# Attention stage of a fused kernel: a fixed engine order, Q's feature map in place on PSUM or on ScalarE, another queue for the s stores, gated FFN loads

## Chip, cores, metric

The kernel runs on 1 core of one Trainium2 chip. The metric is device time in microseconds (us) of one execution. All executions count as fast (within 1.5% of the kernel's fastest), but for one of e5.

## The reference

```python
xn = layernorm(x)                                   # x: 2048 tokens x 1024, bf16
# A: linear attention, 32 heads of 32
q, k, v = split(xn @ wqkv)
phi = lambda t: where(t > 0, t + 1, exp(t)) + 1e-6
kv = einsum("bhsd,bhse->bhde", phi(k), v);  z = sum_s phi(k)
o  = (phi(q) @ kv) / (phi(q) @ z + 1e-6)
s  = o @ wo
# B: gated FFN, F = 3584
g  = silu((silu(xn @ w_gate) * (xn @ w_up)) @ w_down)
out = x + s * g
```

Since `phi(t) = min(exp(t), 1) + max(t, 0) + 1e-6`, it needs no select.

## The kernel before

The code is cut to what the change touches (cuts are marked, and the comments are added here). There are three stages in time: K/V (all of K and V, and the sums `kv` and `z`), attention (Q, numerator/denominator "ND", the transposition of o to oT, and S = oT times wo), and the FFN. Tokens come in four blocks `b` of 512, with four tiles `t` each. GpSimd computes in the background, from the FFN weights, difference tiles T that the FFN needs ("preparations": a weight load, four tensor operations, two stores to DRAM).

```python
    psA = p12.enter_context(tc.tile_pool(name="psA", bufs=3, space=PSUM))
    psB = p12.enter_context(tc.tile_pool(name="psB", bufs=3, space=PSUM))   # q_ps, s_ps, kv_ps
    psC = p12.enter_context(tc.tile_pool(name="psC", bufs=2, space=PSUM))

    def emit_phi(work, t_ps, dst, W, in_place=False):
        e_t = work.tile([P, W], FP32, name="e_t", tag="e_t")
        ex = nc.scalar.activation(out=e_t[:], in_=t_ps, func=ACT.Exp)
        if in_place:                       # used by K from tile 9 on
            r = t_ps
            nc.vector.tensor_scalar(out=r, in0=t_ps, scalar1=0.0, scalar2=EPS, op0=ALU.max, op1=ALU.add)
        else:                              # used by Q
            r_t = work.tile([P, W], FP32, name="r_t", tag="r_t")
            r = r_t[:]
            nc.scalar.activation(out=r, in_=t_ps, func=ACT.Relu)
            nc.vector.tensor_scalar(out=r, in0=r, scalar1=EPS, scalar2=None, op0=ALU.add)
        nc.vector.scalar_tensor_tensor(out=dst, in0=e_t[:], scalar=1.0, in1=r,
                                       op0=ALU.min, op1=ALU.add)
    # ... cut
    def prep(n, after=None):               # one preparation: weight load (SP queue), then GpSimd
        # ... cut
            t = w_slot()
            load_gu(t, key[1], key[2], after)
            emit_T(key, t)                 # 4 gpsimd.tensor_tensor, 2 gpsimd DMA stores
    # ... cut: K/V stage, with one prep per token tile from tile 10 on
        emit_C(NT - 1)
        p1_man.close()                     # end of the explicit order: the scheduler decides from here
        for g in range(G):
            emit_Q(0, g)                   # 8 matmuls of 512 columns, then emit_phi(...)
            if g % 4 == 3:
                prep(1)
    # ... cut
        def emit_OT(b, hf):                # o of two tiles to DRAM, and back transposed
            nc.sync.dma_start(out=rows..., in_=o_blk[:, hf * th:(hf + 1) * th, :])
            nc.sync.dma_start_transpose(out=oT_tiles[b][:, :, hf * tk:(hf + 1) * tk], in_=rows)

        def emit_S(b, t, cc):              # 8 matmuls, one ScalarE copy
            # ... cut
            if cc == NCC - 1:
                nc.gpsimd.dma_start(out=s_dram[r0:r0 + P, :], in_=s_tiles.pop((b, t))[:])

        for b in range(NB):                # fq: Q(b+1), then S(b-1)
            # ... cut
            fill(2)
            for t in range(TPB):
                emit_ND(b, t)
                fill(1 if lastb else 2)
                if t % 2 == 1:
                    emit_OT(b, t // 2)
                    prep(1)
            if b + 1 < NB:
                fill(max(0, len(fq) - 4))
                prep(1)
        # ... then S of what is left, and of the last block
```

Of the kernel before, what the change touches and what calls it, by code (L numbers as in the profile page):

```python
# [21 lines left out]
def kernel(  # L22
# [12 lines left out]
    P = 128  # L35
# [37 lines left out]
    tp = ctx.enter_context(tc.tile_pool(name="tp", bufs=8))  # L73
    p12 = ExitStack()
    psA = p12.enter_context(tc.tile_pool(name="psA", bufs=3, space=PSUM))
    psB = p12.enter_context(tc.tile_pool(name="psB", bufs=3, space=PSUM))
    psC = p12.enter_context(tc.tile_pool(name="psC", bufs=2, space=PSUM))

    SCHED = mybir.DependencyInfo(mybir.DependencyClass.NoSync, mybir.DependencyReason.SCHED_ONLY)
    SYNCD = mybir.DependencyInfo(mybir.DependencyClass.Sync, mybir.DependencyReason.SCHED_ONLY)  # L80
# [45 lines left out]
    def blk_rows_pt(t_dram, b):  # L126
        return t_dram[b * TB:(b + 1) * TB, :].rearrange("(t p) d -> p t d", p=P)

    def emit_phi(work, t_ps, dst, W, in_place=False):
        e_t = work.tile([P, W], FP32, name="e_t", tag="e_t")  # L130
        ex = nc.scalar.activation(out=e_t[:], in_=t_ps, func=ACT.Exp)  # L131
        if in_place:
            r = t_ps
            nc.vector.tensor_scalar(out=r, in0=t_ps, scalar1=0.0, scalar2=EPS, op0=ALU.max, op1=ALU.add)
        else:
# [3 lines that stand above are left out]
            nc.vector.tensor_scalar(out=r, in0=r, scalar1=EPS, scalar2=None, op0=ALU.add)  # L139
        nc.vector.scalar_tensor_tensor(out=dst, in0=e_t[:], scalar=1.0, in1=r,  # L140
                                       op0=ALU.min, op1=ALU.add)
        return ex

    blk12_es = ExitStack()
    blk12 = blk12_es.enter_context(tc.tile_pool(name="blk12", bufs=2, side="right"))
# [4 lines left out]
    def emit_Q(b, g):  # L150
        if b not in pqT_tiles:
            pqT_tiles[b] = blk12.tile([P, G, TB], BF16, name="pqT", tag="pqT")
        pqT = pqT_tiles[b]
        btok = slice(b * TB, (b + 1) * TB)
        q_ps = psB.tile([P, TB], FP32, name="q_ps", tag="B")
        for dc in range(DC):
            nc.tensor.matmul(q_ps[:], lhsT=wq_sb[:, dc, g * P:(g + 1) * P], rhs=xn_ap(dc, btok),  # L157
                             start=(dc == 0), stop=(dc == DC - 1))
        emit_phi(phiw, q_ps[:], pqT[:, g, :], TB)

    NPASS = NB // 2
    passes = list(range(NPASS - 1, -1, -1))
# [8 lines left out]
    w_tiles = {}  # L171
    w_next = [0]
    n_slot = [0]

    def w_slot():
        t = wgu.tile([P, DC, FW], BF16, name="w_sb", tag=("wg_sb" if n_slot[0] % 2 == 0 else "wu_sb"))
# [3 lines left out]
    def load_gu(t, kind, k, after=None):  # L180
        d = nc.sync.dma_start(out=t[:], in_=(wg_v if kind == "g" else wu_v)[:, :, k * FW:(k + 1) * FW])
        gate([d], after, sync=True)

    def load_w(after=None):
        key = w_seq[w_next[0]]
        w_next[0] += 1
        if key in w_tiles:
            return
        p, kind, k = key
        t = w_slot()  # L190
        if kind[0] == "d":
            nc.sync.dma_start(out=t[:].rearrange("p a b -> p (a b)").rearrange("p (k n) -> p k n", k=2),
                              in_=wd_v[:, 2 * k:2 * k + 2, :])
        else:
            load_gu(t, kind, k, after)
        w_tiles[key] = t

    def load_w_to(n):
# [24 lines left out]
    def load_T(key):  # L223
        ta, tb = t_pair()
        for dst, src in zip((ta, tb), t_drams[key[1:]]):
            nc.sync.dma_start(out=dst[:].bitcast(FP32), in_=src[:])
        t_tiles[key] = (ta[:, 1], ta[:, 0], tb[:, 0], tb[:, 1])

    gkeys = [(passes[0], kd, fg) for fg in range(NFG) for kd in ("g", "u")]
# [2 lines left out]
    def prep(n, after=None):  # L232
        for _ in range(n):
            if not prep_q:
                return
            key = prep_q.popleft()
            t = w_slot()
            load_gu(t, key[1], key[2], after)
            emit_T(key, t)
            if key in gkeys[0:2]:  # L240
                w_tiles[key] = t
            else:
                t_tiles.pop(key)

    kvz_ps = [psA.tile([P, GPT, NDW], FP32, name=f"kvz{j}", tag="A") for j in range(NJ)]
    with ExitStack() as p1:
# [248 lines left out]
            if i >= 10:  # L495
                prep(1)
        emit_C(NT - 1)
        p1_man.close()
        for g in range(G):
            emit_Q(0, g)  # L500
            if g % 4 == 3:
                prep(1)

    for j in range(NJ):
        g0 = j * GPT
        ng = min(GPT, G - g0)
        nc.vector.tensor_tensor(out=KVZ[:, g0:g0 + ng, 0:P], in0=kvz_ps[j][:, 0:ng, 0:P],
                                in1=mask[:, None, :].to_broadcast([P, ng, P]), op=ALU.mult)
        nc.vector.tensor_tensor(out=KVZ[:, g0:g0 + ng, P:P + HPG],
                                in0=kvz_ps[j][:, 0:ng, P:P + 1].to_broadcast([P, ng, HPG]),  # L510
                                in1=sel[:, None, :].to_broadcast([P, ng, HPG]), op=ALU.mult)
# [17 lines left out]
    with ExitStack() as p2:  # L529
# [9 lines left out]
        def emit_ND(b, t):  # L539
            pqT = pqT_tiles[b]  # L540
            ttok = slice(t * P, (t + 1) * P)
            if b not in o_blks:
                o_blks[b] = blk.tile([P, TPB, D], BF16, name="o_blk", tag="o_blk")
            o_sb = o_blks[b][:, t, :]
            for j in range(NJ):
                g0 = j * GPT
                ng = min(GPT, G - g0)
                pool_j = psC if j == NJ - 1 and NJ > 1 else psA
                nd_ps = pool_j.tile([P, GPT, NDW], FP32, name="nd_ps", tag=("C" if pool_j is psC else "A"))
                for gi in range(ng):  # L550
                    g = g0 + gi
                    mm = nc.tensor.matmul(nd_ps[:, gi, :], lhsT=pqT[:, g, ttok], rhs=KVZ[:, g, :],  # L552
                                          start=True, stop=True)
                    if j == 0 and gi == 0 and t == 0:
                        marks[("ND", b)] = mm
                rden = small.tile([P, GPT, HPG], FP32, name="rden", tag="rden")
                nc.vector.tensor_scalar(out=rden[:, 0:ng, :], in0=nd_ps[:, 0:ng, P:P + HPG],
                                        scalar1=EPS, scalar2=None, op0=ALU.add)
                nc.vector.reciprocal(out=rden[:, 0:ng, :], in_=rden[:, 0:ng, :])
                nc.vector.tensor_tensor(  # L560
                    out=o_sb[:, g0 * P:(g0 + ng) * P].rearrange("p (g h e) -> p g h e", g=ng, h=HPG),
                    in0=nd_ps[:, 0:ng, 0:P].rearrange("p g (h e) -> p g h e", h=HPG),
                    in1=rden[:, 0:ng, :, None].to_broadcast([P, ng, HPG, DH]),
                    op=ALU.mult)
# [10 lines left out]
        def emit_S(b, t, cc):  # L575
            oT = oT_tiles[b]
            ttok = slice(t * P, (t + 1) * P)
            if (b, t) not in s_tiles:
                s_tiles[(b, t)] = work.tile([P, D], BF16, name="s_sb", tag="s_sb")
            s_sb = s_tiles[(b, t)]  # L580
            s_ps = psB.tile([P, CW], FP32, name="s_ps", tag="B")
            for c in range(G):
                nc.tensor.matmul(s_ps[:], lhsT=oT[:, c, ttok], rhs=wo_sb[:, c, cc * CW:(cc + 1) * CW],  # L583
                                 start=(c == 0), stop=(c == G - 1))
            nc.scalar.copy(out=s_sb[:, cc * CW:(cc + 1) * CW], in_=s_ps[:])  # L585
            if cc == NCC - 1:
                r0 = b * TB + t * P
                nc.gpsimd.dma_start(out=s_dram[r0:r0 + P, :], in_=s_tiles.pop((b, t))[:])  # L588

        fq = deque()  # L590

        def fill(n):
            for _ in range(n):
                if not fq:
                    return
                fq.popleft()()

        for b in range(NB):
            if b + 1 < NB:
                for g in range(G):  # L600
                    fq.append(lambda b=b + 1, g=g: emit_Q(b, g))
            if b > 0:
                for t in range(TPB):
                    for cc in range(NCC):
                        fq.append(lambda b=b - 1, t=t, cc=cc: emit_S(b, t, cc))
            lastb = b == NB - 1
            fill(2)
            for t in range(TPB):
                emit_ND(b, t)
                fill(1 if lastb else 2)  # L610
                if t % 2 == 1:
                    emit_OT(b, t // 2)
                    prep(1)
            if b + 1 < NB:
                fill(max(0, len(fq) - 4))
                prep(1)
        blk_es.close()
        blk12_es.close()
        sp = ctx.enter_context(tc.tile_pool(name="p3S", bufs=1, side="right"))
        emit_Ssum(passes[0])  # L620
        prep(len(prep_q))
        while fq:
            fq.popleft()()
        for t in range(TPB):
            for cc in range(NCC):
                emit_S(NB - 1, t, cc)
    p12.close()

    with ExitStack() as p3:
# [138 lines left out]
        with tc.manual_schedule(engines={mybir.EngineType.PE, mybir.EngineType.DVE, mybir.EngineType.Activation,  # L768
                                         mybir.EngineType.Pool}):
            base = 0  # L770
            for pi, p in enumerate(passes):
# [4 lines left out]
                def get_T(key):  # L776
# [4 lines left out]
                    else:  # L781
                        emit_T(key, w_tiles[key])

                load_w_to(base + 5)
                for i in range(3):
                    get_T(keys[i])
                emit_a(keys[0])
                emit_c22(keys[0])
                for i in range(n):
# [46 lines left out]
```

## Time and profile before

| | before |
|---|---|
| time, median | 830.1 us (829.65 to 830.28) |
| span of the profiled execution | 828.0 us |
| first Q matmul / first FFN matmul | 134.2 / 275.7 us |
| attention, from one to the other | 141.5 us |
| FFN, to the end of the span | 552.3 us |

PE is TensorE, DVE VectorE, ACT ScalarE, POOL GpSimd, SPq the queue of SyncE from which most DMAs are issued. From the page of the kernel before, the busy share in tenths in 40 slices of 20.7 us, and the clock that TensorE was granted:

```profile
PE   6999999579999999999999999999999999999997
DVE  6675436999556276676776027076676776710405
POOL 2471799930101145345380001020000000000200
PEclk9999999769999999999999999999999999999999
```

The two slices with a 5 and a 7 for PE are 145 to 186 us; DVE shows 9 in both, POOL 9 and then 3, and PEclk 7 and 6. The table of stretches gives the same in us (columns: stretch, its length, busy us of each engine with its instruction count, granted clock, DMA share, GB/s):

```profile
140.00:160.00 20.00, 13.27 (x46) 5.11 (x46) 19.90 (x8) 4.34 (x8) 19.94 (x22) 0.77 0.84 291
160.00:180.00 20.00, 11.56 (x45) 4.88 (x44) 18.48 (x27) 6.12 (x12) 13.27 (x15) 0.63 0.60 234
179.20:276.00 96.80, 96.22 (x527) 47.82 (x536) 60.98 (x181) 42.66 (x74) 8.14 (x15) 1.00 0.43 128
```

TensorE is idle or slow in the first two stretches, and full from 179 us on. The chain of waits, in order of time, says who holds it (start, us, what):

```profile
140.22 3.75 DVE r_t L139
...
144.69 5.96 DVE r_t L139
...
151.36 3.75 DVE r_t L139
...
155.83 5.94 DVE r_t L139
...
173.22 6.00 PE q_ps L157 x16
```

These are VectorE's "+EPS" additions to r_t. The same operation on 512 elements takes 0.43 us in the group's median, not 6 us. The last line shows sixteen matmuls in 6.00 us, which take 3.45 us at full clock. The timeline shows what ran beside one of them (start, us, engine, line, operation, out<-in, count):

```profile
144.61 6.03 DVE L139 TENSOR_SCALAR r_t<-r_t 128x512 f32<-128x512 f32 x1
144.75 1.17 POOL L212 TENSOR_TENSOR T_1910<-w_sb 128x512 fp32r<-128x512 bf16 x1
...
145.86 1.16 POOL L214 TENSOR_TENSOR T_1911<-w_sb 128x512 fp32r<-128x512 bf16 x1
...
146.97 1.16 POOL L213 TENSOR_TENSOR T_1910<-w_sb,T_1910 128x512 fp32r<-128x512 bf16 x1
148.09 1.15 POOL L212 TENSOR_TENSOR T_2063<-w_sb 128x512 fp32r<-128x512 bf16 x1
149.20 1.15 POOL L215 TENSOR_TENSOR T_1911<-w_sb,T_1910 128x512 fp32r<-128x512 bf16 x1
...
150.67 0.69 DVE L140 SCALAR_TENSOR_TENSOR pqT<-e_t,r_t 128x512 bf16<-128x512 f32 x1
```

The 6.03 us addition ends 0.3 us after a run of five GpSimd tensor operations has ended (150.64 and 150.35 us), while the K/V stage's in-place form, with its operand in PSUM, isn't touched by the same neighbour (count, then min/median/max in ns):

```profile
L134 DVE TENSOR_SCALAR kv_ps<-kv_ps x14: 700/700/700, 85.0 to 131.4; 128x512 f32<-128x512 f32 x14
```

### The profile page before, as it was taken

The numbers are of one execution on the slowest core, as the hardware profiler recorded it, in microseconds if no ns is written. First come the engines' busy times: TensorE is split into PE (matmuls) and PEld (weight loads), VectorE is DVE, ScalarE is ACT, GpSimd is POOL, SyncE is SP. The second block draws the span as 40 slices with busy tenths as digits, with TensorE's granted clock in tenths as the row PEclk, the third lists the DMA queues.
The fourth block names the chain that finished last, engine by engine and source line by source line (L and its number), as shares of the span: only waits on it lengthen the run. The fifth ranks groups of instructions, "written<-read, shape, count | busy, mean of one in ns | idle before, by whom it ended". The sixth has DMA issues, their size and how long they took to land.

```text
span 828.0 us, 10023 instructions
## 1 busy us (share of the span) xinstructions
PE 794.4 (96%) x3736; PEld 434.3 (52%) x3808; DVE 475.1 (57%) x728; ACT 221.5 (27%) x364; POOL 214.4 (26%) x325
## 2 busy tenths in 40 slices
PE   6999999579999999999999999999999999999997
PEld 3544444135544666666665444456666666644443
DVE  6675436999556276676776027076676776710405
ACT  4544333245343322322222011032322222200102
POOL 2471799930101145345380001020000000000200
PEclk9999999769999999999999999999999999999999
DMA  9249978834525377877878538569777777754541
GB/s 325 82 150 228 308 274 283 314 145 130 153 89 178 115 245 237 275 230 242 272 232 294 181 118 320 165 189 364 252 247 252 247 258 241 252 200 152 204 152 51
DMA packets 149760, 178.92 MB, mean 216 GB/s; under 512 B 30928, under 2 KB 106064, under 8 KB 149712
## 3 DMA queue, kind: packets, MB, share of 16 engines
q1 hardware_dynamic: 137984, 137.25, 52.3%
q0 software_dynamic: 11584, 40.90, 13.8%
q8 instruction: 30, 0.49, 0.2%
q10 hardware_dynamic: 144, 0.13, 0.1%
q14 instruction: 18, 0.15, 0.1%
HBM read 127.93 MB, written 44.04 MB: 208 GB/s over the span
## 4 chain that ended last, share of the span: by engine, by line
PE 87%; DVE 7%; DMA 3%; POOL 2%; issue 1%; ACT 1%; DVEq 0%; ACTq 0%
PE zw L641 25%; PE xb L641 12%; PE y_pd L726 11%; PE y_ps L726 11%; PE kv_ps L408 9%; PE s_ps L583 7%; PE yb L641 6%; PE q_ps L157 5%; DVE r_t L139 3%; DMA xnT<-xn_dram 1%; DMA xn_dram<-xn_blk 1%; PE nd_ps L552 1%; DVE pqT L140 1%; DVE sy L763 0%; DVE stats L322 0%
## 5 line engine op out<-in xcount | busy, mean ns | idle before, releaser
L726 PEld LDWEIGHTS <-hT 128*128 128x128 bf16 x896 | 87.7, 98 | 105.7
L408 PE MATMUL kv_ps<-wkv_sb,xnT 128*128 128x512 bf16 x499 | 114.3, 383 | 2.1 <-DMA xnT<-xn_dram 1.5
L641 PE MATMUL xb<-xnT,w_sb 128*128 128x512 bf16 x420 | 113.7, 380 | 1.5
L726 PE MATMUL y_ps<-w_sb,hT 128*128 128x512 bf16 x440 | 102.5, 379 | 0.4
L726 PE MATMUL y_pd<-w_sb,hT 128*128 128x512 bf16 x438 | 102.0, 379 | 0.5
L763 DVE TENSOR_TENSOR sy<-sy,io 128x512 f32<-128x512 f32 (+1 forms) x33 | 22.2, 671 | 137.6 <-ACT sy L762 137.4
L641 PEld LDWEIGHTS <-w_sb 128*128 128x128 bf16 x672 | 56.8, 98 | 83.1 <-issue 30.5
L766 POOL DMA_DIRECT2D out_dram<-io x24 | 13.0, 543 | 332.5 <-DVE io L764 329.8
L408 PEld LDWEIGHTS <-xnT 128*128 128x128 bf16 x512 | 49.6, 98 | 59.2 <-DMA xnT<-xn_dram 1.9
L157 PE MATMUL q_ps<-xnT,wq_sb 128*128 128x512 bf16 x250 | 64.2, 410 | 10.1 <-ACT r_t L138 9.6
L583 PE MATMUL s_ps<-wo_sb,oT 128*128 128x512 bf16 x249 | 56.0, 379 | 0.4
L698 ACT ACTIVATE sg<-sg 128x1024 f32<-128x1024 f32 x28 | 29.6, 1058 | 97.1 <-DVE sg L694 97.1
L139 DVE TENSOR_SCALAR r_t<-r_t 128x512 f32<-128x512 f32 x50 | 46.0, 920 | 15.4 <-ACT r_t L138 15.1
L762 ACT ACTIVATE sy<-y_pd 128x512 f32<-128x512 f32 x16 | 8.7, 595 | 159.9 <-PE y_pd L726 159.9
L704 DVE TENSOR_TENSOR hT<-cu,sg 128x1536 bf16<-128x1536 f32 x28 | 49.9, 1781 | 0.0
L157 PEld LDWEIGHTS <-wq_sb 128*128 128x128 bf16 x256 | 26.1, 104 | 42.5 <-issue 18.9
L583 PEld LDWEIGHTS <-oT 128*128 128x128 bf16 x256 | 24.8, 98 | 28.8
L588 POOL DMA_DIRECT2D s_dram<-s_sb x16 | 8.7, 543 | 95.4 <-ACT s_sb L585 95.4
L131 ACT ACTIVATE e_t<-q_ps 128x512 f32<-128x512 f32 x32 | 19.1, 597 | 50.2 <-DVE pqT L140 26.0
L641 PE MATMUL zw<-S_2699,w_sb 128*128 128x512 f16 x112 | 29.0, 382 | 0.0
L641 PE MATMUL zw<-S_4632,w_sb 128*128 128x512 f16 x112 | 29.0, 382 | 0.0
L585 ACT CAST s_sb<-s_ps 128x512 bf16<-128x512 f32 x32 | 18.7, 586 | 35.1 <-PE s_ps L583 32.0
(1000 smaller groups left out, 1221.5 us busy)
## 6 DMA issues: line engine op xcount, KB each, us to landing
w_sb<-in_B_w_down_dram SPq DMA_DIRECT2D x56, 512.0 KB, 4.0
w_sb<-in_B_w_gate_dram SPq DMA_DIRECT2D x40, 512.0 KB, 5.2
w_sb<-in_B_w_up_dram SPq DMA_DIRECT2D x28, 512.0 KB, 5.7
o_dram<-o_blk SPq DMA_DIRECT2D x8, 512.0 KB, 2.8
s_dram<-s_sb POOLq DMA_DIRECT2D x16, 256.0 KB, 2.3
io<-in_A_x_dram SPq DMA_DIRECT2D x16, 256.0 KB, 3.4
io<-s_dram SPq DMA_DIRECT2D x16, 256.0 KB, 4.1
xp<-in_A_x_dram SPq DMA_DIRECT2D x15, 256.0 KB, 7.6
```

The lines of the kernel that those rows point to most:

```text
L131: ex = nc.scalar.activation(out=e_t[:], in_=t_ps, func=ACT.Exp)
L139: nc.vector.tensor_scalar(out=r, in0=r, scalar1=EPS, scalar2=None, op0=ALU.add)
L157: nc.tensor.matmul(q_ps[:], lhsT=wq_sb[:, dc, g * P:(g + 1) * P], rhs=xn_ap(dc, btok), start=(dc == 0), stop=(dc == DC - 1))
L408: mm = nc.tensor.matmul(kv_ps[:], lhsT=xn_ap(dc, tok), rhs=wkv_sb[:, dc, c * CW:(c + 1) * CW], start=(dc == 0), stop=(dc == DC - 1))
L583: nc.tensor.matmul(s_ps[:], lhsT=oT[:, c, ttok], rhs=wo_sb[:, c, cc * CW:(cc + 1) * CW], start=(c == 0), stop=(c == G - 1))
L585: nc.scalar.copy(out=s_sb[:, cc * CW:(cc + 1) * CW], in_=s_ps[:])
L641: nc.tensor.matmul(out, lhsT=lhs(k), rhs=rhs(k), start=(first and k == 0), stop=(k == HK - 1), skip_group_check=True)
L698: nc.scalar.activation(out=c[:, 1:3, :], in_=c[:, 1:3, :], func=ACT.Silu)
L704: nc.vector.tensor_tensor(out=hv[:, TB:4 * TB], in0=c[:, 1:4, :].rearrange("p a b -> p (a b)"), in1=sg[:, 1:4, :].rearrange("p a b -> p (a ...
L726: nc.tensor.matmul(ys[(t, c)], lhsT=h[:, fc, tt], rhs=wt[:, o:o + CW], start=(fc == 0), stop=(fc == FC - 1), skip_group_check=True)
L763: nc.vector.tensor_tensor(out=sy[:], in0=sy[:], in1=s_in[:, cs], op=ALU.mult)
L766: eng.dma_start(out=out2[r0:r0 + P, cs], in_=xres[:, cs])
```

## The change

Its intent: no VectorE operation of Q's feature map that GpSimd can lock out; VectorE's load cut in half where ScalarE has room; the whole attention stage in a fixed order, with S(b-1) spread between Q(b+1), and the preparations one by one after each o transposition; the s stores off GpSimd's queue; and the first FFN loads held back until S of the last block begins.

```diff
-    def emit_phi(work, t_ps, dst, W, in_place=False):
+    def emit_phi(work, t_ps, dst, W, in_place=False, act=False):
         e_t = work.tile([P, W], FP32, name="e_t", tag="e_t")
-        ex = nc.scalar.activation(out=e_t[:], in_=t_ps, func=ACT.Exp)
+        if act:
+            nc.scalar.activation(out=e_t[:], in_=t_ps, func=ACT.Relu, scale=-1.0)
+            nc.scalar.activation(out=e_t[:], in_=e_t[:], func=ACT.Exp, scale=-1.0)
+            nc.scalar.activation(out=t_ps, in_=t_ps, func=ACT.Relu)
+            nc.vector.scalar_tensor_tensor(out=dst, in0=e_t[:], scalar=EPS, in1=t_ps,
+                                           op0=ALU.add, op1=ALU.add)
+            return
+        nc.scalar.activation(out=e_t[:], in_=t_ps, func=ACT.Exp)
# emit_Q: psB (3 buffers) becomes ps2 (5 buffers, shared with S and a third of ND), and
-        emit_phi(phiw, q_ps[:], pqT[:, g, :], TB)
+        emit_phi(phiw, q_ps[:], pqT[:, g, :], TB, in_place=True, act=b > 0 or g % 2 == 1)
# ... cut
-            load_gu(t, kind, k, after)
+            load_gu(t, kind, k, after or first_gate[0])
# ... cut: the same gate on the first T loads
+    p2_man.enter_context(tc.manual_schedule(engines={PE, DVE, Activation, Pool, SP}))   # all of attention
# ... cut
-                nc.gpsimd.dma_start(out=s_dram[r0:r0 + P, :], in_=s_tiles.pop((b, t))[:])
+                nc.scalar.dma_start(out=s_dram[r0:r0 + P, :], in_=s_tiles.pop((b, t))[:])
# ... cut: fq and fill are replaced by a list
+        for b in range(NB):
+            q = [q_item(b + 1, g) for g in range(G)] if b + 1 < NB else []
+            sl = sh(b - 1, 0) + sh(b - 1, 1) if b > 0 else []          # the 8 S items of block b-1
+            body = q[:2] + mix(q[2:], sl)
+            at = (1, 4, 7, 10) if len(body) > 12 else ((1, 3, 5, 7) if b == 0 else (0, 1, 2, 3))
+            for k, f in enumerate(body):
+                f()
+                if k in at:
+                    nd_item(b, at.index(k))()       # ND; after an odd tile also emit_OT and prep(1)
# ... cut: then S of the last block
+                if pi == 0:
+                    first_gate[0] = marks[("S", NB - 1, 0)]
                 load_w_to(base + 5)
```

More of the change, by code (lines that the diff above doesn't have):

```diff
@@ L75 @@
     psA = p12.enter_context(tc.tile_pool(name="psA", bufs=3, space=PSUM))
-    psB = p12.enter_context(tc.tile_pool(name="psB", bufs=3, space=PSUM))
-    psC = p12.enter_context(tc.tile_pool(name="psC", bufs=2, space=PSUM))
+    ps1 = ExitStack()
+    psB = ps1.enter_context(tc.tile_pool(name="psB", bufs=3, space=PSUM))
+    psC = ps1.enter_context(tc.tile_pool(name="psC", bufs=2, space=PSUM))
     SCHED = mybir.DependencyInfo(mybir.DependencyClass.NoSync, mybir.DependencyReason.SCHED_ONLY)
@@ L141, in emit_phi @@
                                        op0=ALU.min, op1=ALU.add)
-        return ex
     blk12_es = ExitStack()
@@ L154, in emit_Q @@
         btok = slice(b * TB, (b + 1) * TB)
-        q_ps = psB.tile([P, TB], FP32, name="q_ps", tag="B")
+        q_ps = ps2.tile([P, TB], FP32, name="q_ps", tag="B2")
         for dc in range(DC):
@@ L173 @@
     n_slot = [0]
+    first_gate = [None]
     def w_slot():
@@ L225, in load_T @@
         for dst, src in zip((ta, tb), t_drams[key[1:]]):
-            nc.sync.dma_start(out=dst[:].bitcast(FP32), in_=src[:])
+            gate([nc.sync.dma_start(out=dst[:].bitcast(FP32), in_=src[:])], first_gate[0], sync=True)
         t_tiles[key] = (ta[:, 1], ta[:, 0], tb[:, 0], tb[:, 1])
@@ L497 @@
         emit_C(NT - 1)
-        p1_man.close()
+        ps1.close()
+        ps2 = p12.enter_context(tc.tile_pool(name="ps2", bufs=5, space=PSUM, reuse_waits="tile"))
         for g in range(G):
@@ L502 @@
                 prep(1)
+        p1_man.close()
+    p2_man = ExitStack()
+    p2_man.enter_context(tc.manual_schedule(engines={mybir.EngineType.PE, mybir.EngineType.DVE,
+                                                     mybir.EngineType.Activation, mybir.EngineType.Pool,
+                                                     mybir.EngineType.SP}))
     for j in range(NJ):
@@ L547, in emit_ND @@
                 ng = min(GPT, G - g0)
-                pool_j = psC if j == NJ - 1 and NJ > 1 else psA
-                nd_ps = pool_j.tile([P, GPT, NDW], FP32, name="nd_ps", tag=("C" if pool_j is psC else "A"))
+                if j < NJ - 1:
+                    nd_ps = psA.tile([P, GPT, NDW], FP32, name="nd_ps", tag="A")
+                else:
+                    nd_ps = ps2.tile([P, GPT, NDW], FP32, name="nd_ps2", tag="B2")
                 for gi in range(ng):
@@ L580, in emit_S @@
             s_sb = s_tiles[(b, t)]
-            s_ps = psB.tile([P, CW], FP32, name="s_ps", tag="B")
+            s_ps = ps2.tile([P, CW], FP32, name="s_ps", tag="B2")
             for c in range(G):
-                nc.tensor.matmul(s_ps[:], lhsT=oT[:, c, ttok], rhs=wo_sb[:, c, cc * CW:(cc + 1) * CW],
-                                 start=(c == 0), stop=(c == G - 1))
+                mm = nc.tensor.matmul(s_ps[:], lhsT=oT[:, c, ttok], rhs=wo_sb[:, c, cc * CW:(cc + 1) * CW],
+                                      start=(c == 0), stop=(c == G - 1))
+                marks.setdefault(("S", b, t), mm)
             nc.scalar.copy(out=s_sb[:, cc * CW:(cc + 1) * CW], in_=s_ps[:])
@@ L587, in emit_S, with q_item, s_item, nd_item @@
                 r0 = b * TB + t * P
-                nc.gpsimd.dma_start(out=s_dram[r0:r0 + P, :], in_=s_tiles.pop((b, t))[:])
-        fq = deque()
-        def fill(n):
-            for _ in range(n):
-                if not fq:
-                    return
-                fq.popleft()()
-        for b in range(NB):
-            if b + 1 < NB:
-                for g in range(G):
-                    fq.append(lambda b=b + 1, g=g: emit_Q(b, g))
-            if b > 0:
-                for t in range(TPB):
-                    for cc in range(NCC):
-                        fq.append(lambda b=b - 1, t=t, cc=cc: emit_S(b, t, cc))
-            lastb = b == NB - 1
-            fill(2)
-            for t in range(TPB):
+                nc.scalar.dma_start(out=s_dram[r0:r0 + P, :], in_=s_tiles.pop((b, t))[:])
+        def q_item(b, g):
+            return lambda: emit_Q(b, g)
+        def s_item(b, t, cc):
+            return lambda: emit_S(b, t, cc)
+        def nd_item(b, t):
+            def f():
                 emit_ND(b, t)
-                fill(1 if lastb else 2)
                 if t % 2 == 1:
@@ L613, with mix, sh @@
                     prep(1)
-            if b + 1 < NB:
-                fill(max(0, len(fq) - 4))
-                prep(1)
+            return f
+        def mix(a, b_):
+            r = []
+            for k in range(max(len(a), len(b_))):
+                r += a[k:k + 1] + b_[k:k + 1]
+            return r
+        def sh(b, hf):
+            return [s_item(b, t, cc) for t in (2 * hf, 2 * hf + 1) for cc in range(NCC)]
+        for b in range(NB):
[7 more added lines that the diff above has]
+                    nd_item(b, at.index(k))()
+        b = NB - 1
         blk_es.close()
@@ L621 @@
         prep(len(prep_q))
-        while fq:
-            fq.popleft()()
-        for t in range(TPB):
-            for cc in range(NCC):
-                emit_S(NB - 1, t, cc)
+        for f in sh(b, 0) + sh(b, 1):
+            f()
+    p2_man.close()
     p12.close()
@@ L786 @@
                     get_T(keys[i])
+                first_gate[0] = None
                 emit_a(keys[0])
```

## The prediction

> **What bounds the kernel now.** The chain of waits is 87% TensorE; for the FFN (276 us to 828 us of the span) it is almost nothing else. The exception is the start of attention. Between 137.7 and 173 us the chain's pieces are VectorE's: the "+EPS" TENSOR_SCALAR on r_t, eight times 1.3 to 6.0 us, where its group's median is 0.43 us, and the pqT SCALAR_TENSOR_TENSOR after it. The table of stretches shows TensorE busy 13.3 and 11.6 of 20 us in 140-160 and 160-180, with its clock at 0.77 and 0.63. GpSimd is busy 19.9 and 13.3 of 20 us there: its weight-preparation TENSOR_TENSORs were pulled forward by the scheduler. In the timeline each slow TENSOR_SCALAR ends within 0.4 us of the end of a run of GpSimd tensor operations. The Trainium skill ("SBUF — State Buffer", "Who interferes with whom") says that VectorE in a 2-port mode, or with two SBUF inputs, and GpSimd lock each other out, and that one SBUF input outside such a mode doesn't contend. The trace agrees: the K/V stage's in-place version on PSUM takes 700 ns in all 14 instances, with GpSimd busy beside it.
>
> From 179.2 to 276 us TensorE is 99% busy at full clock: 416 matmuls of 512 columns at 0.216 us plus 15 numerator groups of 0.47 us make 96.9 us, the whole stretch.
>
> **What the change does.**
> - Q's feature map: the 50% of block 0 in place costs VectorE 0.70 + 0.69 us; the rest has one VectorE operation (0.69 us) and three ScalarE ones (about 0.6 us, the second waiting for the first: estimate 1.6 to 1.8 us per group, against 1.73 us of matmuls). No VectorE operation has two SBUF inputs or a 2-port form any more. ScalarE is tight in Q(1) only.
> - Explicit order: preparations 9 to 14 no longer run before attention but after each o transposition, so GpSimd is mostly idle during Q(0).
> - s stores leave GpSimd's queue for ScalarE's.
> - S(b-1) is spread between Q(b+1). oT must arrive earlier: for the first S item I estimate 1 to 3 us of slack (store 2.8 us + transposition 4.2 us after VectorE's 2.7 us), for block 3's first half 0.5 to 1.5 us.
> - FFN loads wait for S of the last block, about 14 us before the FFN: enough for first use.
>
> **Sum.** Attention's TensorE work is 512 x 0.216 + 16 x 0.47 = 118 us. It should start at about 135.2 us (after the last K/V matmuls) and end at about 253.2 us, with 1 to 2 us of small waits at 254.7, where now it ends at 276. Saved: 21.5 us, all on the critical path. Predicted 808.5 us, range 805.5 to 815; faster by over 2% 0.86, within 2% 0.13, slower 0.01.
>
> **What would show it.** TensorE's clock tenths stay at 9 throughout; no VectorE operation in Q(0) over 1 us; about 80 Q matmuls done by 153 us instead of 173; first FFN matmul near 254 us; FFN length unchanged at about 552 us; GpSimd's tensor work in 140-160 us nearly gone.
>
> **What would make it wrong.** S waiting for oT (strict order can't fill that hole); ScalarE's dependent chain taking over 2 us per group, so that Q(1) waits for PSUM; the late GpSimd preparations colliding with the S sums (two SBUF inputs) before the FFN; gated loads arriving late, which would lengthen the FFN's start by several us.

## The result, and the profile after

| | before | after |
|---|---|---|
| time, median | 830.1 us | 815.72 us (814.78 to 817.15) |
| ratio | 1 | 0.9829 (0.981 to 0.9848) |
| first Q / first FFN matmul | 134.2 / 275.7 us | 135.3 / 260.6 us |
| attention | 141.5 us | 125.3 us |
| FFN | 552.3 us | 552.4 us |

A ratio is the mean time of one kernel's fast runs over that of the other's of the same rounds, so it is not quite the ratio of the medians. All outputs are right. The kernel is 1.7% faster, where 2.6% was predicted; 815.7 us lies just outside the range of 805.5 to 815.

The span starts with loads and the K/V stage, which end at slightly different times from one execution to the next (the first Q matmul lies between 134.2 and 139.3 us in all traces but the slow one of e5). Attention's length is therefore the sharper measure. Before it was 141.5 us, and the estimate of pure TensorE work was 118 us.

The slow start is gone. The page's rows of the changed kernel for TensorE and its clock:

```profile
PE   6999999999989999999999999999999999999997
PEclk9999999999998999999999999999999999999999
```

and its stretches:

```profile
140.00:160.00 20.00, 20.00 (x107) 9.55 (x105) 12.50 (x26) 15.46 (x28) 0.00 (x0) 1.00 0.00 0
...
240.00:260.00 20.00, 15.35 (x63) 6.43 (x62) 8.99 (x4) 6.49 (x9) 3.92 (x4) 0.83 0.94 265
```

TensorE is full in 140 to 160 us, at full clock; but 240 to 260 us shows 15.35 of 20 us and a clock of 0.83, which the kernel before did not have. The chain of waits names it:

```profile
161.88 3.90 DMA o_dram<-o_blk
...
165.80 5.19 DMA oT<-o_dram
...
171.03 1.90 PE s_ps L600 x8
...
233.33 3.44 PE s_ps L600 x16
236.77 8.07 DMA oT<-o_dram
...
244.89 16.09 PE s_ps L600 x64
```

Twice the chain runs through the o store and the transposition of oT. At 171 us this is nearly free. At 240.2 us TensorE has done the last S item of block 2 and stands until 244.89 us, since the first half of oT of block 3 lands only then, 8.07 us after its issue. TensorE's waits in this stage (total us, times, longest):

```profile
PE s_ps L600 <- DMA oT<-o_dram: 5.1, 2, 4.7
```

After the hole the clock is down: 64 matmuls take 16.09 us, against 64 x 0.216 = 13.8 us, so 2.3 us more. The stretches show it (columns as above; the granted clock is the third number from the end):

```profile
242.00:244.00 2.00, 0.00 (x0) 0.00 (x0) 0.00 (x0) 0.00 (x0) 0.00 (x0) 0.59 1.21 219
244.00:246.00 2.00, 1.11 (x3) 0.43 (x4) 0.00 (x0) 0.00 (x0) 0.00 (x0) 0.50 1.09 398
...
250.00:252.00 2.00, 2.00 (x11) 0.91 (x10) 2.00 (x2) 0.59 (x1) 0.00 (x0) 1.00 0.88 191
```

The queue's issues around the hole (SPq timeline):

```profile
231.88 0.38 SPq L589 DMA_DIRECT2D o_dram<-o_blk  x1
236.77 4.30 SPq L590 DMA_TRANSPOSE oT<-o_dram  x1
241.58 0.65 SPq L589 DMA_DIRECT2D o_dram<-o_blk  x1
```

The o store of 231.88 took 4.9 us before the transposition could be issued, where before such stores took 2.8 us in the median. While the two were under way, from 231.9 to 244.8 us, so were two T stores of 0.5 MB that GpSimd had issued from 226.3 us on, two more from 236.3 us on, four s stores, and the o store of the second half; the weight load of 224.88 us had landed at 231.6 us.

The sum for attention: 118 us of work, 0.4 us at the first S item, 4.65 us of hole and 2.3 us of low clock make 125.35 us; the trace has 125.3 us.

### The profile page after: what moved, and what is told of

Same layout as the page of the kernel before. It is cut to its first block, busy times and chain, and to the rows that moved or that the text cites. A ratio compares the mean times of both kernels' runs of the same rounds, so it can differ in the third digit from the quotient of the medians.

```text
span 813.0 us, 10086 instructions
## 1 busy us (share of the span) xinstructions
PE 792.4 (97%) x3808; PEld 432.4 (53%) x3808; DVE 446.0 (55%) x700; ACT 236.9 (29%) x388; POOL 205.0 (25%) x309
## 4 chain that ended last, share of the span: by engine, by line
PE 88%; DMA 5%; DVE 3%; POOL 2%; issue 1%; ACT 1%; SPq 0%; DVEq 0%
PE zw L663 25%; PE xb L663 12%; PE y_pd L748 12%; PE y_ps L748 11%; PE kv_ps L417 8%; PE s_ps L600 7%; PE yb L663 6%; PE q_ps L165 4%; DMA oT<-o_dram 2%; DMA xnT<-xn_dram 1%; DMA xn_dram<-xn_blk 1%; DMA xp<-in_A_x_dram 1%; PE kvz L439 1%; PE nd_ps L569 1%; DVE sy L785 0%
## 5 line engine op out<-in xcount | busy, mean ns | idle before, releaser
L663 PE MATMUL zw<-S,T 128*128 128x512 f32 x672 | 175.3, 409 | 0.0
L663 PEld LDWEIGHTS zw<-S,T 128*128 128x128 f32 x672 | 126.4, 188 | 32.3
L682 ACT COPY s<-xb 128x512 f32<-128x512 f32 x56 | 32.7, 584 | 158.4 <-PE xb L663 158.4
L221 POOL TENSOR_TENSOR T<-w_sb 128x512 fp32r<-128x512 bf16 x28 | 32.5, 1161 | 175.1 <-DMA w_sb<-in_B_w_gate_dram 80.2
L683 DVE TENSOR_TENSOR s<-yb,s 128x512 f32<-128x512 f32 x56 | 38.6, 689 | 63.9 <-ACT s L682 63.9
L663 PE MATMUL yb<-S,T 128*128 128x512 f32 x224 | 71.5, 441 | 0.0
L600 PE MATMUL s_ps<-wo_sb,oT 128*128 128x512 bf16 x256 | 60.1, 389 | 5.1 <-DMA oT<-o_dram 5.1
L165 PE MATMUL q_ps<-xnT,wq_sb 128*128 128x512 bf16 x256 | 58.2, 379 | 0.0
L663 PE MATMUL zw<-S,w_sb 128*128 128x512 f16 x224 | 58.0, 382 | 0.0
L684 DVE TENSOR_TENSOR s<-zw,s 128x512 f32<-128x512 f32 x56 | 38.7, 692 | 26.6 <-PE zw L663 26.5
```

Source lines behind the costliest of these rows:

```text
L165: nc.tensor.matmul(q_ps[:], lhsT=wq_sb[:, dc, g * P:(g + 1) * P], rhs=xn_ap(dc, btok), start=(dc == 0), stop=(dc == DC - 1))
L221: nc.gpsimd.tensor_tensor(out=T1, in0=b12, in1=b11, op=ALU.subtract)
L600: mm = nc.tensor.matmul(s_ps[:], lhsT=oT[:, c, ttok], rhs=wo_sb[:, c, cc * CW:(cc + 1) * CW], start=(c == 0), stop=(c == G - 1))
L663: nc.tensor.matmul(out, lhsT=lhs(k), rhs=rhs(k), start=(first and k == 0), stop=(k == HK - 1), skip_group_check=True)
L682: nc.scalar.copy(out=s1[:], in_=x_[:])
L683: nc.vector.tensor_tensor(out=s2[:], in0=y_[:], in1=s1[:], op=ALU.add)
```

## The experiments

The questions: what made the start fast, the feature map or the order; and why does oT come late, because of too much traffic, the wrong queue, or too little slack in the fixed order. All runs are compared in this table. Attention and the waits are from the profiled execution. Each group of rounds has its own runs of the kernel before on the same chip, with medians of 829.5 to 830.1 us.

| run | edit, against | time, median us | ratio to before | attention us | TensorE waits for oT, us |
|---|---|---|---|---|---|
| after | | 815.72 | 0.9829 | 125.3 | 5.1 |
| after_again | none, the changed kernel again | 814.09 | 0.981 | 124.8 | 4.1 |
| e1_phi_only | before + feature map | 807.1 | 0.9723 | 118.2 | 0 |
| e2_order_only | after - feature map | 818.93 | 0.9865 | 130.2 | 4.7 |
| e3_preps_in_q0 | after, preparations earlier | 813.72 | 0.9802 | 123.3 | 3.6 |
| e4_s_on_gpsimd | after, s stores on GpSimd | 818.43 | 0.9855 | 126.4 | 0.7 |
| e5_no_gate | after - gate | 828.22 | 0.9965 | (see below) | |
| e5b_no_gate | the same | 827.6 | 0.9964 | 137.7 | 15.0 |
| e6_slack | after, more slack | 807.68 | 0.9741 | 117.8 | 0 |
| e7_preps_in_q0_s_later | e3, first S later | 808.51 | 0.9748 | 117.8 | 0 |
| e8_psum_only | before + PSUM form alone | 810.32 | 0.9763 | 120.1 | 0 |
| e9_slack_and_preps | e6 and e3 | 806.74 | 0.9731 | 117.8 | 0 |

### e1_phi_only

The kernel before with nothing changed but Q's feature map.

```diff
# in the kernel before: the new emit_phi, and in emit_Q
-        emit_phi(phiw, q_ps[:], pqT[:, g, :], TB)
+        emit_phi(phiw, q_ps[:], pqT[:, g, :], TB, in_place=True, act=b > 0 or g % 2 == 1)
```

> The kernel before with the new feature map of Q alone (PSUM in place or on ScalarE); the scheduler still pulls the GpSimd preparations before attention, and TensorE's order stays. Theory L (the slow start was VectorE's 2-port TENSOR_SCALAR locked out by GpSimd): no VectorE operation between 135 and 175 us over 1 us although GpSimd is busy there, Q(0) ends near 149.5 us instead of 166; time 808 to 816 us, the upper part if the three PSUM buffers of Q and S, now held until VectorE is done, make TensorE wait. Theory O (it was the order and the timing of the preparations that had to change): the start stays slow, 824 us or more.

Measured: 807.1 us (805.68 to 808.12), ratio 0.9723 (0.9708 to 0.9737). This is 1.1% faster than the changed kernel, a single part of it. Its stretch from 140 to 160 us:

```profile
140.00:160.00 20.00, 20.00 (x106) 9.55 (x104) 13.65 (x32) 14.92 (x28) 19.94 (x23) 1.00 0.79 274
```

GpSimd is as busy as in the kernel before (19.94 of 20 us), and TensorE is full at full clock all the same. VectorE beside GpSimd in its timeline:

```profile
142.25 1.15 POOL L221 TENSOR_TENSOR T<-w_sb 128x512 fp32r<-128x512 bf16 x1
...
143.36 1.16 POOL L222 TENSOR_TENSOR T<-w_sb,T 128x512 fp32r<-128x512 bf16 x1
143.68 0.69 DVE L135 SCALAR_TENSOR_TENSOR pqT<-e_t,q_ps 128x512 bf16<-128x512 f32 x1 [1.34 <-ACT e_t L133]
...
144.38 0.70 DVE L141 TENSOR_SCALAR q_ps<-q_ps 128x512 f32<-128x512 f32 x1
```

The longest of Q's VectorE operations takes 0.70 us, so theory L holds in what it says of the time: the start was slow because of the form of VectorE's operation, and it did not need another order. (That the old form was a 2-port mode, as the expectation has it, no record shows: the trace doesn't name an operation's mode.) TensorE doesn't wait at all in 125 to 300 us, also not for the three PSUM buffers, which had been feared. With 118.2 us the attention stage is at the estimate of 118 us of pure work. Its transfers were not quick: the first o store took 11.9 us to land beside the preparations' traffic, and TensorE still waited for no oT. The order that the scheduler chose leaves room for that.

### e2_order_only

The changed kernel with Q's old feature map: the order, the queue and the gate alone.

```diff
-        emit_phi(phiw, q_ps[:], pqT[:, g, :], TB, in_place=True, act=b > 0 or g % 2 == 1)
+        emit_phi(phiw, q_ps[:], pqT[:, g, :], TB)
```

> The changed kernel with Q's old feature map (Relu on ScalarE into SBUF, VectorE adds EPS from SBUF to SBUF). Theory L: no slow start, since GpSimd is idle in Q(0) in this order (0.43 us for each TENSOR_SCALAR), but in 172-237 us, beside GpSimd's six spread preparations, some TENSOR_SCALARs take 1 to 5 us each; VectorE falls behind, oT comes later, 816 to 824 us. Theory O: the order alone gives all of the gain, 814 to 817 us, with no VectorE operation over 2 us.

Measured: 818.93 us (817.69 to 820.27), ratio 0.9865 (0.9848 to 0.9881), within the range of theory L and outside that of O. In 140 to 160 us GpSimd is idle (0.00 us) and the stage starts at full speed. At 172 us, beside the first of the later preparations, VectorE and GpSimd again slow each other:

```profile
172.13 1.68 DVE L148 SCALAR_TENSOR_TENSOR pqT<-e_t,r_t 128x512 bf16<-128x512 f32 x1
...
173.34 1.49 POOL L222 TENSOR_TENSOR T<-w_sb,T 128x512 fp32r<-128x512 bf16 x1
...
173.74 1.38 DVE L147 TENSOR_SCALAR r_t<-r_t 128x512 f32<-128x512 f32 x1
```

Operations of 0.43 and 0.69 us take 1.38 to 1.68 us; TensorE waits 3.8 us for VectorE's o_blk and again 4.7 us for oT. So the order also cures the start, by moving GpSimd's work away from it, but that work then has to be paid for somewhere else. The two parts don't add up: each removes the same stall, which is why the order was worth so little on top of the feature map (and, as the medians of e1 and the changed kernel show, cost 8.6 us). The collision is weaker than the 4 to 6 us of the kernel before. That kernel has the weak form too: its last two slow additions, at 166.86 and 169.94 us, took 1.59 and 1.37 us, ending 0.3 us after a single GpSimd operation, where the long ones outlasted three (3.8 us) or five (6.0 us). What decides how many VectorE has to sit out is not settled.

### e3_preps_in_q0

The changed kernel leaves GpSimd idle for 39 us (133 to 172 us) and has preparations during the late transpositions. Here they come at once:

```diff
             emit_Q(0, g)
-            if g % 4 == 3:
-                prep(1)
+            prep(1)
```

> The changed kernel, with the remaining six weight preparations emitted in Q(0) instead of after each o transposition: GpSimd and the DMA queues work through 133-170 us, where the changed kernel leaves them idle, and are free of it in 170-240 us. Theory C (the 5 us hole before S of the last block, and its cold clock, come from the preparations' loads and stores sharing the DMA engines with the o store and transposition): o store back to 2.8-3.6 us, transposition to 4.2-5 us, TensorE's wait for oT under 1 us, FFN starts near 254 us; 807 to 810 us. Rival D (the order alone leaves too little work between the last block's second numerator and its first S item): the hole stays at 3 us or more and the time above 812 us. Rival Q (it is the s stores on ScalarE's queue that slow the transposition): the hole stays too.

Measured: 813.72 us (812.76 to 814.25), ratio 0.9802 (0.9788 to 0.9817): neither theory's number. The trace splits the answer. The last block's hole is gone, its store lands in 2.9 us and its transposition in 4.2 us, as theory C said:

```profile
161.39 0.38 SPq L588 DMA_DIRECT2D o_dram<-o_blk  x1
166.95 3.59 SPq L589 DMA_TRANSPOSE oT<-o_dram  x1
...
236.32 0.38 SPq L588 DMA_DIRECT2D o_dram<-o_blk  x1
239.20 1.82 SPq L589 DMA_TRANSPOSE oT<-o_dram  x1
```

But the first o store (161.39) now shares the DMA engines with the preparations' last stores: 5.6 us to the transposition's issue, 6.8 us for the transposition, and TensorE waits 3.6 us at the first S item instead. The hole has followed the traffic. That rules out rival D for the last block (TensorE's order is the same, and there is no hole) and rival Q as well (the s stores are still on ScalarE's queue, so its hole would have stayed); which transposition is late follows the preparations. It also shows that the first S item has too little slack: the two transfers took 5.4 us more than 2.8 + 4.2 us, and TensorE waited 3.6 us of it.

The traces also say which traffic it is likely to be. In the twelve of them at full speed (all but e5's), each of the 17 transpositions that took 5.9 us or more (up to 10.3 us) had GpSimd's T stores under way beside it, the 59 with none took 4.1 to 5.8 us, and the 20 others, mostly beside T stores for a shorter time, 4.3 to 5.6 us. This is a coincidence in time and not an experiment: s stores and weight loads were often there as well.

### e4_s_on_gpsimd

```diff
-                nc.scalar.dma_start(out=s_dram[r0:r0 + P, :], ...)
+                nc.gpsimd.dma_start(out=s_dram[r0:r0 + P, :], ...)
```

> The changed kernel with the s stores back on GpSimd's queue. Rival Q (the s stores on ScalarE's queue slow the last block's transposition): the hole shrinks by 3 us or more, time 809 to 812 us. Theory C: the stores are the same bytes on the same DMA engines, so the hole stays within 1.5 us of 4.7 us and the time within 2 us of the changed kernel's 815.7 us; late s stores don't matter, as they are read much later.

Measured: 818.43 us (815.97 to 819.04), ratio 0.9855 (0.9839 to 0.9871). Rival Q's time is refuted: the kernel is not faster. The transposition of the last block's first half still takes 7.0 us. The wait for oT did shrink to 0.7 us, but only because TensorE had been held up before it by something else:

```profile
PE nd_ps L569 <- ACT s_sb L603: 3.7, 1, 3.7
PE s_ps L600 <- ACT s_sb L603: 0.9, 1, 0.9
```

In a fixed order a store on GpSimd's queue stands behind a preparation that waits for its weights; the s_sb buffers fill up, ScalarE waits for one (11.3 us in all), and PSUM isn't freed. So in this order the s stores had to leave GpSimd's queue, though little depends on it: 2.7 us of the medians, and the two intervals of the ratio overlap. What the move alone does to the kernel before was not run.

### e5_no_gate and e5b_no_gate

```diff
-                    first_gate[0] = marks[("S", NB - 1, 0)]
+                    pass
```

> The changed kernel without the gate on the first FFN loads. Reading of the trace: in the changed kernel those loads leave the queue 0.1 us after the last o transposition's issue, 4 us after the instruction they wait for, so the queue's order and not the gate times them. Expected: same trace, hole before S of the last block 4 to 6 us, time within 0.3% of the changed kernel's 815.7 us. If the gate protected the transposition, the hole would grow and the time pass 818 us.

Measured: 828.22 us (827.73 without the slow execution), ratio 0.9965 (0.9941 to 0.9988): nearly all of the gain lost. The expectation was wrong: in the changed kernel the gate looks idle, as its loads leave only after the last transposition. One of the four executions took 2138 us, and it was the profiled one: 32 matmuls took 19.05 us there, 0.595 us each, with a granted clock of 1.00 in the records, while VectorE's operations took their usual time (0.69 us for pqT). It did not recur in the other three or in the four of e5b, it is not used, and it stays unexplained. The list of instructions then showed what the gate does besides waiting: the FFN's loads are outside the fixed order, and without the gate the scheduler places them before the o stores of blocks 2 and 3.

> The same kernel as the one without the gate, for a profile in the ordinary state (its only profile fell on an execution with TensorE at less than half speed). The list of instructions now shows that without the gate the scheduler, which still places the queue's FFN loads, puts two of them before block 2's second o store and five before block 3's first. Theory G (the gate keeps FFN loads from blocking the queue in front of o stores): o stores leave late by several us behind a load that waits for a free buffer, TensorE waits for oT over 10 us in all; 824 to 829 us. If it is only bandwidth: o stores leave on time but land late. One more execution at double length would show that it belongs to this kernel; none would leave it unexplained.

Measured: 827.6 us (825.65 to 828.06), ratio 0.9964 (0.9947 to 0.9982), attention 137.7 us. The queue around block 3's first half:

```profile
231.85 5.29 SPq L190 DMA_DIRECT2D w_sb<-in_B_w_up_dram  x3
237.25 2.78 SPq L235 DMA_DIRECT2D T<-t_g  x2
240.12 0.39 SPq L589 DMA_DIRECT2D o_dram<-o_blk  x1
249.41 4.32 SPq L590 DMA_TRANSPOSE oT<-o_dram  x1
```

VectorE finishes that half's o at 231.6 us; the store leaves at 240.12 us, 8.5 us late, behind three weight loads and two T loads. Then it takes 9.2 us to land and the transposition 7.4 us more. TensorE waits 15.0 us for oT, 10.5 us of it here. So both act: the queue, as theory G said (8.5 us late), and transfers that land late (16.7 us for the two, against 7.0 us in the kernel before's medians). The gate is not an extra gain: it undoes damage that the fixed order with unfixed loads would have.

### e6_slack

The preparations stay where the changed kernel has them. Only the distance between a transposition and its first reader grows:

```diff
+        late = []                  # ahead of the loop over blocks
-            sl = sh(b - 1, 0) + sh(b - 1, 1) if b > 0 else []
-            body = q[:2] + mix(q[2:], sl)
+            late += sh(b - 1, 0) + sh(b - 1, 1) if b > 0 else []
+            n_s = len(late) if b == NB - 1 else max(0, len(late) - 2)
+            sl, late = late[:n_s], late[n_s:]
+            body = q[:4] + mix(q[4:], sl)
```

> The changed kernel with the preparations where they are, but with more matmuls between an o transposition and its first reader: the first S item two Q groups later (3.5 us), and the last two S items of each block carried into the next, so that ten S items instead of eight lie before the last block's. DMA load is unchanged. Theory T (a fixed order with too little slack meets late transfers; either more slack or shorter transfers cures it): no TensorE wait for oT over 0.5 us, clock full throughout, FFN starts near 253.5 us, 806 to 809 us, although transfers stay as slow. Rival (TensorE's share of the loss is something else, or the DMA merely falls behind for good): a hole of 2 us or more somewhere, 811 us or more.

Measured: 807.68 us (806.45 to 810.12), ratio 0.9741 (0.9723 to 0.9759). The transfers are nearly as slow as in the changed kernel, up to 7.1 us for a transposition (8.1 us there), and nobody waits for them:

```profile
PE kvz L439 <- ACT v_sb L432: 0.4, 1, 0.4
```
```profile
DMA to landing us min/median/max: 4.3/4.6/7.1
```

The first fence is all of TensorE's waits in 125 to 300 us; the second is the time to landing of the eight transpositions. Theory T holds, and the rival (the DMA falls behind for good) falls.

### e7_preps_in_q0_s_later

e3 with `body = q[:4] + mix(q[4:], sl)`, so that the first S item comes two Q groups later.

> The earlier variant with all preparations in Q(0), whose hole of 3.6 us had moved to the very first S item, with that item two Q groups (3.5 us) later. Theory T: the first hole shrinks to under 0.5 us, none opens elsewhere as the transfers of the last block are quick here; 806.5 to 809 us. Rival: the hole reopens at another S item; 811 us or more.

Measured: 808.51 us (807.02 to 812.25), ratio 0.9748 (0.9722 to 0.9774). No wait for oT is left; attention takes 117.8 us. The profiled execution was the slowest of the four (812.25 us), since its K/V stage ended late (first Q at 139.3 us).

### e8_psum_only

e1 with `in_place=True` and no ScalarE form.

> The kernel before with only the PSUM in-place form of the feature map for every Q group, without the ScalarE form: VectorE then does 0.70 + 0.69 us per group, 1.39 us, beside 2.7 us per numerator tile: 5.5 us per two Q groups and one numerator, against 3.9 us of TensorE. If the lock-out alone mattered: like the feature map alone, 806 to 809 us. If moving work to ScalarE matters too: VectorE falls behind in Q(1) and Q(2), with three PSUM buffers TensorE waits for VectorE 3 us or more in 153-210 us, 810 to 818 us.

Measured: 810.32 us (808.19 to 812.63), ratio 0.9763 (0.9742 to 0.9785); attention 120.1 us against 118.2 us in e1. GpSimd is as busy as before in 140 to 160 us, and VectorE is full in 160 to 180 us:

```profile
140.00:160.00 20.00, 19.84 (x103) 9.57 (x105) 17.25 (x36) 6.64 (x12) 19.94 (x23) 1.00 0.79 279
160.00:180.00 20.00, 19.57 (x122) 10.26 (x122) 19.89 (x60) 5.63 (x10) 14.18 (x16) 1.00 1.05 360
```

TensorE waits 1.1 us in three places, 0.6 us of it for VectorE. So the PSUM form alone brings most of the gain, 21.4 of 23.3 us of attention, and ScalarE's form some 2 us more. The time is at the lower edge of the second branch, but the waits are less than the 3 us that it named.

### after_again

> The changed kernel once more, on the same chip as the next two, so that the gate and the slack are judged beside it. Expected 814.5 to 817.5 us, with the hole before S of the last block 4 to 6 us.

Measured: 814.09 us, with executions of 811.92, 811.92, 816.25 and 816.32 us, ratio 0.981 (0.978 to 0.9839). Just under the range expected, with a wait for oT of 4.1 us, 4.0 us of it at one place, in the profiled execution of 816.25 us. The two quick executions have a mean granted clock of 0.999, against 0.995 and 0.997 for the slow two. So they ran at low clock for less time, and the hole was probably shorter in them; they were not profiled.

### e9_slack_and_preps

> Both cures together, more slack and the preparations in Q(0). Theory T: nothing is left to gain from TensorE's waits in attention, so it equals the better of the two and the feature map alone, 806 to 808.5 us. Under 805 us would mean a further loss that the traces of those have hidden.

e6 with e3's edit. Measured: 806.74 us (806.38 to 810.57), ratio 0.9731 (0.9707 to 0.9756), attention 117.8 us. It equals e6 and e1 within their intervals. Nothing is left to gain from TensorE's waits in attention. The fastest versions, e1, e6 and e9, beat both kernels, and e1 is by far the smallest edit.

## Why the prediction was right or wrong

- **What bounds the kernel: right.** TensorE, except for the lock-out at the start of attention. e1 shows it: GpSimd as busy as before, the stall gone.
- **The feature map's costs: right.** ScalarE's groups of three operations follow each other in 1.73 us from 151 to 155 us, as fast as TensorE's, and TensorE didn't wait for them; no VectorE operation in Q(0) takes over 0.70 us; the 80th Q matmul was done near 153 us.
- **TensorE's work in attention, 118 us: right.** e1, e6, e7 and e9 measure 117.8 to 118.2 us. The FFN's 552 us was right too.
- **"oT must arrive earlier: ... for block 3's first half 0.5 to 1.5 us" of slack: wrong, and this is the step that failed.** It was computed with the kernel before's latencies, store 2.8 us and transposition 4.2 us. In that trace the preparations were over before the first o store, so these were latencies of quiet DMA engines. The same text moved the preparations into that very stretch, and didn't price the traffic: it became 4.9 and 8.1 us, 6.0 us more. The slack was as estimated for the quiet latencies: the store of o began at 231.88 us, 7.0 us later is 238.88 us, and TensorE ran dry at 240.24 us, 1.36 us after that. So the term that failed is the latency, 7.0 us assumed and 13.0 us measured. e3 shows the quiet latencies coming back when the traffic is away, e6 shows that with slack the slow ones do no harm.
- **"1 to 2 us of small waits": mis-sized.** The hole of 4.65 us was followed by 2.3 us of matmuls at a lower clock. The kernel before's profile had shown this very effect (6.00 us for sixteen matmuls). The Trainium skill ("TensorE: Matmul & The Clock Gate", "What's actually happening") says that an idle window of about 3.4 us halves the clock and that as long a busy one restores it. The trace agrees that the clock halves and comes back: the records give 0.50 in 244 to 248 us, and 1.00 again in 250 to 252 us. It doesn't agree in the times: the clock fell near 242.4 us, some 2.1 us after TensorE's last matmul, and stayed down for 6.8 us (both worked out from the mean clocks of the stretches). Such a wait should have been costed with one window at half speed on top: an estimate of 1.7 us from that page's 3.4 us, where the trace has 2.3 us.
- **Listed under what would make it wrong, and right there: "S waiting for oT (strict order can't fill that hole)".** Of the others, none cost TensorE time in the trace: it waited for nothing but oT in 140 to 300 us, and the FFN takes as long as before.
- **The gain was credited to the whole change; the runs credit one part.** Feature map alone 0.9723, all of it 0.9829. The fixed order, with its preparations and its tight oT, gave 7 us of attention back; the gate repairs what that order would break (e5b), and so, for a few us at most, does the queue change (e4).

On queues: the Trainium skill ("DMA: Bandwidth & Descriptors", "Queues, rings and completion order") says that the queues of SP and ScalarE have rings on the same sixteen DMA engines, and that each engine takes turns between the queues it has work for. e4 agrees as far as it goes: with the stores on another queue the transposition of the last block's first half took 7.0 us instead of 8.1 us, still far from 4.2 us. Which of the transfers hurts the transposition most was not measured one by one.

## What to carry to other kernels

Before you reorder, look at the form of the operation that stalls: keeping one intermediate (r) in PSUM instead of SBUF brought 21.4 us of attention here, with GpSimd just as busy (e8), and a new order of five engines with the old form 11.3 us (e2). A latency read from the trace holds for the traffic of that stretch; if the change moves transfers into it, take the loaded latency (here 8.1 us for 4.2 us in the changed kernel, and 11.9 us for a store of 2.8 us in e1) and give a fixed order that much slack, since it can't fill a hole. A hole can cost TensorE's clock as well: in the attention stage of these traces, every stop of TensorE of 3.1 us or more had a granted clock of 0.50 during or after it, and the one of 1.7 us in e2 had not; no stop of a length in between began at full clock. Test a bundle of changes part by part: parts that remove the same stall don't add up, and some are there only to repair others.

## What the Trainium skill lacked or had wrong

- "SBUF — State Buffer", "Who interferes with whom", says that whoever issues first gets the shared ports for the whole instruction, and that the other waits until that one has finished. That the pair contends is confirmed (0.43 us became 1.4 to 6.0 us; with PSUM for an operand, Q's operations took at most 0.70 us). But a VectorE operation whose record began at 144.61 us ended only after five GpSimd tensor operations in a row had (6.03 us), so the wait can last many instructions; in e2 the same pair cost only 1.4 to 1.7 us. Who was first is not clear: the five began at 144.75 us, but a DMA issue of GpSimd's was under way from 144.19 to 144.72 us.
- "DMA: Bandwidth & Descriptors" gives a bandwidth for the DMA transposition, but no time to landing for one beside other transfers: 0.5 MB took 4.2 us in quiet stretches, up to 8.1 us beside stores in the changed kernel, and up to 10.3 us beside stores and loads in e5b.
- No page has an execution that is slow from start to end as e5's is (it would belong to "TensorE: Matmul & The Clock Gate"): matmuls of 512 columns some 0.6 us apart (32 in 19.05 us), 2138 us in all, with a granted clock of 1.00 in the records.
